# A new way to the first scores, a whole last copy and a new order table in an attention + SwiGLU kernel

## The chip, the core and the metric

The kernel runs on one core of a Trainium2 chip. Its engines are TensorE (PE in the profile; its weight loads are PEld), VectorE (DVE), ScalarE (ACT), GpSimd (POOL) and SyncE (SP), which issues most of the DMAs. The metric is the device time of one execution in microseconds (us); lower is better.

## The reference

With x of 2048 rows and 512 columns, 32 heads of 16, and a feed-forward width of 1792:

```
qkv    = x @ wqkv                                  # q, k, v per head
scores = q @ k.T * 16 ** -0.5                      # 32 heads, 2048 x 2048 each
a      = (softmax(scores) @ v) @ wo
b      = (silu(x @ w_gate) * (x @ w_up)) @ w_down
g      = sigmoid((x * gate_w).sum(-1))
out    = g * a + (1 - g) * b
```

All inputs and the output are bf16.

## The kernel before, in words

**Units and tiles.** Attention is cut into 32 units: four blocks of 512 queries (`QBW`) by eight groups of four heads. A unit has 16 tiles, one for each 128 keys. A tile holds the scores of four heads, 128 keys by 4 x 512 queries, and takes one of two ways:

- On ScalarE: two score pairs. Each is two matmuls into a PSUM tile `s_t` of 128x1024 and one exponential `e_t <- s_t` (`emit_pair`).
- On VectorE: four single scores `d_t` of 128x512. Each is evicted by a multiply-add to 16-bit integers that are read as bf16, which makes an approximate power (`emit_d`). The tile is then finished by whole-tile passes over `c_t` of 128x2048 (class `Pass`), of which GpSimd takes strips of columns (`strip`, `g_now`).

The products with the values go to `o_ps`, one PSUM tile for each unit (`pv`). A finished unit is copied out as `osb` (`post`). Its rows are gathered by DMA into `on`, which is normalised and multiplied by `wo`.

**Other work.** The q, k and v projections, the gate and up products `gu` with one tanh each on ScalarE (56 in all), and the down and output products `dps` and `ops` are chains of small pieces that fill TensorE between the score pairs (`Pacer`, `Chain`, `side`, `put_piece`).

**The order** is fixed when the program is built. A planner runs its own clock for each engine (`plan.pe`, `plan.dve`, `plan.act`, `plan.pool`) with fixed costs: 0.6 us for a VectorE eviction of 512 columns, 0.9167 us for an exponential (`ACT_US`). It decides step by step what each engine gets next. Each engine executes its instructions in that order. `v_unit` gives a tile to VectorE when, by the plan, VectorE would be done with it before ScalarE reaches the end of the unit (`plan.dve + busy + LEAD <= end`). So the number of exponentials is a result of the plan. The table `TURNS` bends the decisions: its letters come in twos for each score pair, the first read by `turn_of`, the second by `way_of`, and a dot changes nothing. For example, `k` or `j` puts value products ahead of other pieces, `h` and `i` move the limit in `v_unit` by 2 us, `v` and `w` change how much work may wait for VectorE, and `q` lets a GpSimd strip take 0.4 us longer. The table before has 131 letters besides the dots, 11 of them `q`.

**The way to the first scores** is written out by hand (L1245 to L1306). `keep_warm` issues products that nobody reads. `turn` transposes `x_rows` (kept in `wd_t`) by products with the identity. The other two of the four 128-column chunks of x come by DMA transposes. Chunk 3 goes to PSUM tile `tp` and is copied by ScalarE in one instruction of 1024 columns; chunk 2 is copied by VectorE in two of 512. Then come 8 matmuls for the keys (`kp0`, 1024 columns), 4 for the queries (`qp0`), and the largest key of each row on VectorE (`largest`, `k_neg`). After 32 small products for the first values (`v0`), `bound_add` adds the bound to `qp0`. VectorE makes two masked copies of the queries (`q0a`, one for each of two head pairs) and a plain one. ScalarE evicts the keys into `kaug` and the values into `vaug`. The first score pair reads `kaug` and the first masked copy. The planner starts after that, with `plan.dve = plan.pe + 3.9` (L1309).

**The end** is also written out by hand (L1765 to L1795). The last unit's `o_ps` is copied in two halves of 256 columns, the first by VectorE, the second by ScalarE (L1132 to L1136). Then `denominators` (tile `dt`), `recip16` and `spread_rows` (tile `rps`) run, four products `on_l = osb * rps`, and the last four matmuls with `wo_l`. The ten products listed in `rest` (tiles `al` and `al_o`) are put between these by `tail(n)`. Four evictions and three output DMAs end the program.

Nearly all instructions go through helpers, so that the profile shows L192 for PE, L195 for ACT and L204 for DVE, POOL and SP; they are told apart by their tiles.

Of the kernel before, what the change touches and what calls it, by code (L numbers as in the profile page):

```python
# [8 lines left out]
ACT = mybir.ActivationFunctionType  # L9
# [44 lines left out]
class Pacer:  # L54
# [33 lines left out]
    "..........s...j.....d........................r.......................q....b...s......l.........l"  # L88
    ".....n.y...f.x....a...b.................k........t............k...h........x...........g....a.s."
    ".......................t..................k...................o................................."  # L90
    "...r......k....................n...................q.....g................k..............r.m...."
    ".........w....................hq..........h...................o......y....d..n..k.....h........."
    "..hqj....xkt.y............a.c.....k....x....c.................................s...........o...j."
    ".......t....j.......i....x......c.s.......e.............j......................................."
    ".....q........................b..f......k.a...b....................................l............"
    "..............o...................................s............................................."
    "..........s........................r..............................................i.........j..."
    "..i............r..............................i............................r.....v........b....."
    ".....q...g..c...b.........h......n...ye..q...q...lc........w............a....w......iq.........."
    "..........b....................n..if.......t....c.............................d..............q.."  # L100
    "...............f.......v....h......u....k..m..cxk........v..................................e..."
    "...f..........j....q..................................o............w............kg.............."
    ".......g..................o"
# [4 lines left out]
def kernel(  # L108
# [176 lines left out]
    for g in (1, 2):  # L285
        ones_rows(nc.vector, g)
# [467 lines left out]
    def emit_pair(bs, ride=0):  # L754
# [1072 lines left out]
```

## Time and profile before

| | us |
|---|---|
| median of 3 runs | 748.87 (747.44 to 748.96) |
| the profiled execution, device time | 748.07 |
| its span, first to last instruction | 746.2 |
| first exponential of the scores starts | 12.92 |
| last exponential of the scores starts | 736.63 |
| last value products end | 738.10 |
| last output DMA is issued | 743.08 |

Busy time in the span: PE 725.7, DVE 724.0, ACT 730.5, POOL 278.5 us. The profile gives each instruction's start and duration; instructions on one engine overlap by a little, so the distance from start to start is what one costs in a dense stretch. The granted clock in the page is 1.00 throughout, but it is recorded only from the first change of clock on; before that, the spacing of the matmuls tells it.

### The profile page before, as it was taken

How to read it: one execution, taken by the hardware profiler on the slowest of the kernel's cores; microseconds unless marked ns; L12 is line 12 of the kernel's file. 1: busy time of each engine (PE TensorE's matmuls, PEld its weight loads, DVE VectorE, ACT ScalarE, POOL GpSimd, SP SyncE). 2: the span in 40 equal slices, each digit the busy share in tenths (PEclk: the TensorE clock that was granted, in tenths of full speed). 3: DMA queues.
4: the chain of work that ended last, by engine and by line, in shares of the span. 5: the costliest groups of instructions: out<-in, count | busy, mean ns of one | idle time of the engine just before them, and what ended most of it. 6: DMA issues, size and time to landing. Idle time of an engine off the chain costs nothing.

```text
span 746.2 us, 22814 instructions
## 1 busy us (share of the span) xinstructions
PE 725.7 (97%) x9173; PEld 214.7 (29%) x9173; DVE 724.0 (97%) x1242; ACT 730.5 (98%) x825; POOL 278.5 (37%) x348
## 2 busy tenths in 40 slices
PE   8999999999999999999999999999999999999997
PEld 3332222222222222322222232222222223222222
DVE  7899999999999999999999999999999999999995
ACT  5999999999999999999999999999999999999996
POOL 5222334333233254444334342342343255354320
PEclk9999999999999999999999999999999999999999
DMA  9000212244210012221100131312001132100001
GB/s 228 8 1 16 53 35 55 58 123 89 60 36 10 20 46 73 61 48 30 37 20 26 31 91 28 78 24 55 20 22 32 48 80 60 32 20 13 15 30 36
DMA packets 91026, 34.44 MB, mean 46 GB/s; under 512 B 75488, under 2 KB 90472, under 8 KB 90920
## 3 DMA queue, kind: packets, MB, share of 16 engines
q1 hardware_dynamic: 89192, 32.66, 18.2%
q8 instruction: 71, 1.16, 0.7%
q10 hardware_dynamic: 1728, 0.33, 0.2%
q14 instruction: 35, 0.29, 0.1%
HBM read 21.55 MB, written 2.35 MB: 32 GB/s over the span
## 4 chain that ended last, share of the span: by engine, by line
PE 54%; ACT 27%; DVE 12%; issue 7%; DMA 0%; ACTq 0%; DVEq 0%
ACT e_t L195 25%; PE s_t L192 18%; PE o_ps L192 15%; DVE c_t L204 7%; PE gu L192 6%; PE ops L192 5%; PE dps L192 2%; ACT th L195 2%; PE qp L192 2%; PE kp L192 2%; PE vp L192 2%; DVE mt L204 1%; DVE kaug L204 1%; DVE gs L204 1%; PE warm L192 1%
## 5 line engine op out<-in xcount | busy, mean ns | idle before, releaser
L195 ACT ACTIVATE e_t<-s_t 128x1024 bf16<-128x1024 f32 x756 | 707.1, 1094 | 1.9 <-PE s_t L192 1.1
L204 DVE TENSOR_SCALAR c_t<-d_t 128x512 uint16<-128x512 f32 x472 | 309.0, 683 | 2.4 <-PE d_t L192 1.9
L192 PE MATMUL s_t<-qx,kaug 32*128 32x512 bf16 (+1 forms) x1188 | 231.3, 384 | 7.9 <-ACT e_t L195 5.8
L204 POOL TENSOR_SCALAR c_t<-c_t 128x1088 uint16<-128x1088 uint16 (+14 forms) x203 | 147.8, 728 | 206.2 <-DVE c_t L204 147.6
L192 PEld LDWEIGHTS <-kaug 32*128 32x128 bf16 (+1 forms) x2048 | 81.9, 91 | 310.1 <-issue 306.2
L192 PE MATMUL o_ps<-e_t,vaug 128*32 128x512 bf16 (+2 forms) x1568 | 149.5, 378 | 0.3 <-DVE vaug L204 0.3
L192 PE MATMUL d_t<-qx,kaug 32*128 32x512 bf16 x444 | 145.3, 384 | 0.0
L192 PE MATMUL o_ps<-c_t,vaug 128*32 128x512 bf16 (+2 forms) x1352 | 121.6, 373 | 0.6 <-DVE vaug L204 0.3
L204 DVE TENSOR_SCALAR c_t<-c_t 128x2048 uint16<-128x2048 uint16 (+7 forms) x181 | 114.8, 646 | 0.5
L204 POOL TENSOR_TENSOR c_t<-c_t 128x480 bf16<-128x480 bf16 (+7 forms) x55 | 61.5, 1128 | 141.3 <-DVE c_t L204 93.3
L192 PEld LDWEIGHTS <-vaug 128*32 128x32 bf16 x3176 | 66.9, 95 | 108.5 <-issue 95.1
L192 PE MATMUL gu<-xT,wg 128*32 128x512 bf16 x896 | 72.2, 383 | 0.0
L192 PE MATMUL gu<-xT,wu 128*32 128x512 bf16 x896 | 67.8, 382 | 0.4
L192 PE MATMUL ops<-wd_t,mt 128*32 128x512 bf16 x672 | 56.5, 382 | 0.0
L204 DVE TENSOR_TENSOR c_t<-c_t 128x1568 bf16<-128x1568 bf16 (+10 forms) x51 | 47.8, 938 | 0.0
L192 PE MATMUL s_t<-q,kaug 32*128 32x512 bf16 (+1 forms) x192 | 37.4, 384 | 2.9 <-ACT e_t L195 2.6
L204 DVE SCALAR_TENSOR_TENSOR mt<-gs,gu 128x512 bf16<-128x512 bf16 x56 | 38.0, 679 | 0.3
L195 ACT ACTIVATE th<-gu 128x512 bf16<-128x512 f32 x56 | 38.2, 682 | 0.0
L204 DVE SCALAR_TENSOR_TENSOR gs<-th,gu 128x512 bf16<-128x512 bf16 x56 | 38.0, 679 | 0.1
L204 DVE TENSOR_SCALAR kaug<-d_t 128x512 uint16<-128x512 f32 x52 | 34.7, 682 | 0.5 <-PE d_t L192 0.5
L204 DVE TENSOR_SCALAR kaug<-c_t 128x2048 uint16<-128x2048 uint16 (+5 forms) x50 | 33.5, 669 | 0.1
L192 PEld LDWEIGHTS <-mt 128*32 128x32 bf16 (+1 forms) x1037 | 24.4, 95 | 26.9 <-issue 20.1
(150 smaller groups left out, 538.0 us busy)
## 6 DMA issues: line engine op xcount, KB each, us to landing
wg<-in_B_w_gate_dram SPq DMA_DIRECT2D x56, 128.0 KB
wu<-in_B_w_up_dram SPq DMA_DIRECT2D x56, 128.0 KB
on<-osb SPq DMA_DIRECT2D x120, 16.0 KB
rb<-rr SPq DMA_DIRECT2D x15, 128.0 KB
wd_t<-in_B_w_down_dram SPq DMA_DIRECT2D x7, 256.0 KB
qx<-qst SPq DMA_DIRECT2D x96, 16.0 KB
qx<-aq SPq DMA_DIRECT2D x96, 16.0 KB
out_dram<-o_t SPq DMA_DIRECT2D x12, 128.0 KB
```

Source lines behind the costliest of these rows:

```text
L192: return ordered(nc.tensor.matmul(*args, **kw))
L195: ordered(nc.scalar.activation(*args, **kw))
L204: return lambda *a, **kw: ordered(f(*a, **kw))
```

## The change

Four parts:

1. **The way to the first scores.** 8 products that nobody reads instead of 12 ahead of the transposing products, 2 instead of 1 behind them. Both transposed chunks are copied in halves, the first 512 rows by VectorE, the second by ScalarE. The memset of `kaug` group 2 (`ones_rows`) moves behind these copies. The keys are made in another order of matmuls, so that the first 512 columns are complete two matmuls earlier; the largest key is taken for each half and merged (`kpart0` has 4 columns). The queries are made in two halves of 256 columns in two PSUM tiles, and the bound is added to each half. One of the four masked half copies goes to ScalarE. The keys are evicted in two halves, the second behind that copy. 6 of the 8 value blocks come ahead of the bound, 2 behind. The eviction of the values moves from ScalarE to VectorE, behind the query copies.
2. **The last copy** of `o_ps` is one ScalarE instruction of 512 columns. For the 30 units between the first and the last, the small constant added in the copy is an immediate instead of a column read from `tiny`.
3. **The last products** in `tail`: 4, 2, 2 and 2 instead of 3, 3, 2 and 2, and the last two come ahead of the fourth of the last matmuls instead of the third.
4. **The table** `TURNS` has other letters throughout: 109 besides the dots, one of them `q`. New letters: `f` and `g` in the first place change the pacer's credit by 1.5, `d` and `o` in the second place let VectorE take a waiting score eviction, or the first due piece, ahead of a pass.

```diff
--- before.py
+++ after.py
@@ -85,22 +85,22 @@
 
 
 TURNS = (
-    "..........s...j.....d........................r.......................q....b...s......l.........l"
...
-    ".......g..................o"
+    ".......v.tbu.d.........r.........................d....b.................................k......."
...
+    ".......................n"
 )
 
 
@@ -282,8 +282,7 @@
             in_=wqk[:, :, i * D:i * D + 64].rearrange("p dc (j c) -> p dc j c", c=DH), func=ACT.Copy)
 
     pad(1)
-    for g in (1, 2):
-        ones_rows(nc.vector, g)
+    ones_rows(nc.vector, 1)
     ident = const.tile([P, P], BF16, name="ident")
     nc.gpsimd.memset(ident[:], 1.0)
     nc.gpsimd.affine_select(out=ident[:], in_=ident[:], pattern=[[-1, P]], compare_op=ALU.is_equal,
@@ -508,15 +507,12 @@
     def k_bound(b):
         vec.tensor_reduce(out=kb[:, b:b + 1], in_=kst[b][:, :], axis=AX.X, op=ALU.max, apply_absolute_value=True)
 
-    def v0(t0):
-
-        p = m_tile("vp")
-        for i in range(8):
+    def v0(p, t0, i0, i1):
+
+        for i in range(i0, i1):
             for dc in range(DC):
                 mm(p[:, 64 * i:64 * i + 64], lhsT=xT[:, dc, (t0 + i) * P:(t0 + i + 1) * P], rhs=wv[:, dc, 0:64],
                    start=(dc == 0), stop=(dc == DC - 1))
-        act(out=v0_out(t0), in_=p[:, :].rearrange("p (t h c) -> p t h c", h=4, c=DH), func=ACT.Copy)
-        m_free(p, 0.0)
 
     def v0_out(t0):
         return vaug[:, t0:t0 + 8, 0:4 * VC].rearrange("p t (h c) -> p t h c", c=VC)[:, :, :, 1:1 + DH]
@@ -777,6 +773,7 @@
         for b in bs:
             e_left[b] = pairs[0]
         pairs[0] += 1
+        pace.credit += {"f": 1.5, "g": -1.5}.get(turn_of(pairs[0]), 0.0)
 
     def turn_of(n):
 
@@ -1022,7 +1019,11 @@
                 j = next((j for j, v in enumerate(vops) if not v.poolable() and v.n // KT <= closed + AHEAD), 0)
                 vops.insert(0, vops.pop(j))
             fit = bool(vops) and not shut and not (code == "u" and vops[0].poolable()) and vops[0].n // KT <= closed + AHEAD and c_ready() <= now
-            if fit and vops[0].key != plan.last and (code == "m" or vops[0].n // KT < au and code != "l"):
+            if code == "d" and d_wait and d_wait[0][0] <= now + 0.05:
+                pay_d()
+            elif code == "o" and due:
+                pay(due[0])
+            elif fit and vops[0].key != plan.last and (code == "m" or vops[0].n // KT < au and code != "l"):
                 pay_v()
             elif d_wait and d_wait[0][2] // KT < au and d_wait[0][0] <= now + 0.05:
                 pay_d()
@@ -1124,18 +1125,14 @@
 
     def post(un):
         qb, g = UNIT[un]
-        if un < UNITS - 1:
-            osbs[un] = osb0[qb] if g == 0 else work.tile([P, QBW], BF16, tag="osb", name="osb")
+        osbs[un] = osb0[qb] if g == 0 else work.tile([P, QBW], BF16, tag="osb", name="osb")
         if un == 0:
             assert part_scaled
             vec.scalar_tensor_tensor(out=osbs[un][:, :], in0=o_of.pop(un)[:, :], scalar=tiny[:, 0:1], in1=o_part, op0=ALU.add, op1=ALU.add)
         elif un == UNITS - 1:
-            o, hw = o_of.pop(un), QBW // 2
-            osbs[un] = [work.tile([P, hw], BF16, tag=t, name="osb")[:, :] for t in ("osb", "th")]
-            vec.tensor_scalar(out=osbs[un][0], in0=o[:, 0:hw], scalar1=tiny[:, 0:1], scalar2=None, op0=ALU.add)
-            act(out=osbs[un][1], in_=o[:, hw:], func=ACT.Identity, bias=tiny[:, 0:1], scale=1.0)
+            act(out=osbs[un][:, :], in_=o_of.pop(un)[:, :], func=ACT.Identity, bias=tiny[:, 0:1], scale=1.0)
         else:
-            vec.tensor_scalar(out=osbs[un][:, :], in0=o_of.pop(un)[:, :], scalar1=tiny[:, 0:1], scalar2=None, op0=ALU.add)
+            vec.tensor_scalar(out=osbs[un][:, :], in0=o_of.pop(un)[:, :], scalar1=TINY, scalar2=None, op0=ALU.add)
 
     def settle(un):
         qb, g = UNIT[un]
@@ -1180,14 +1177,9 @@
                 normed.add((qb, b))
             at.setdefault(n0 + 13 + b, []).append(lambda norm=norm: later(0.345, norm))
 
-    def block(osb, tq):
-        if isinstance(osb, list):
-            osb, tq = osb[tq // 2], tq % 2
-        return osb[:, tq * P:(tq + 1) * P]
-
     def denominators(p, osb):
         for tq in range(TQ):
-            mm(p[:, 4 * tq:4 * tq + 4], lhsT=block(osb, tq), rhs=sel_t[:, :], start=True, stop=True)
+            mm(p[:, 4 * tq:4 * tq + 4], lhsT=osb[:, tq * P:(tq + 1) * P], rhs=sel_t[:, :], start=True, stop=True)
 
     def spread_rows(p, rt):
         for tq in range(TQ):
@@ -1242,15 +1234,13 @@
         return columns(NB + FC, "ops", lambda k: onc[qb][:, k, cs] if k < NB else mt[:, k - NB, cs],
                        lambda k: wo_t[:, k, :] if k < NB else wd_t[:, k - NB, :], lambda p: later(0.65, lambda: end(p)))
 
-    kp0 = ps_s.tile([P, 2 * QBW], F32, tag="s", name="kp0")
-    qp0 = m_tile("qp0")
     warm = ps_o.tile([P, QBW], F32, tag="o", name="warm")
 
     def keep_warm(n):
         for _ in range(n):
             mm(warm[:, :], lhsT=idle[:, 0:P], rhs=idle[:, :], start=True, stop=True)
 
-    kpart0 = const.tile([P, 3], F32, name="kpart0")
+    kpart0 = const.tile([P, 4], F32, name="kpart0")
     kneg0 = mt[:, 3, P:2 * P]
     kneg1 = mt[:, 3, 2 * P:3 * P]
     aq0 = mt[:, 2, :]
@@ -1274,34 +1264,56 @@
             mm(ps[k // TQ][:, k % TQ * P:(k % TQ + 1) * P], lhsT=x_rows[:, k, (dc - HALF) * P:(dc - HALF + 1) * P],
                rhs=ident[:, :], start=True, stop=True)
 
-    keep_warm(12)
+    HQ = QBW // 2
+    fore, aft = slice(0, QBW), slice(QBW, 2 * QBW)
+    keep_warm(8)
     tp = ps_s.tile([P, 2 * QBW], F32, tag="s", name="tp")
-    turn(DC - 1, [tp[:, 0:QBW], tp[:, QBW:2 * QBW]])
-    act(out=xT[:, DC - 1, 0:2 * QBW], in_=tp[:, :], func=ACT.Copy)
+    kp0 = ps_s.tile([P, 2 * QBW], F32, tag="s", name="kp0")
+    tps = [m_tile("tp") for _ in range(2)]
+    for i, dc in enumerate((DC - 1, DC - 2)):
+        turn(dc, [tp[:, i * QBW:(i + 1) * QBW], tps[i]])
+        vec.tensor_copy(out=xT[:, dc, fore], in_=tp[:, i * QBW:(i + 1) * QBW])
+        act(out=xT[:, dc, aft], in_=tps[i][:, :], func=ACT.Copy)
+        m_free(tps[i], 0.0)
     pad(0)
-    tps = [m_tile("tp") for _ in range(2)]
-    turn(DC - 2, tps)
-    for k in range(2):
-        vec.tensor_copy(out=xT[:, DC - 2, k * QBW:(k + 1) * QBW], in_=tps[k][:, :])
-        m_free(tps[k], 0.0)
-    keep_warm(1)
+    ones_rows(vec, 2)
+    keep_warm(2)
     arrived = (3, 0, 2, 1)
-    for dc in arrived:
+    for two in (arrived[:2], arrived[2:]):
         for tb in range(2):
-            mm(kp0[:, tb * QBW:(tb + 1) * QBW], lhsT=wpad[1][:, dc, :], rhs=xT[:, dc, tb * QBW:(tb + 1) * QBW],
-               start=(dc == arrived[0]), stop=(dc == arrived[-1]))
-    for dc in arrived:
-        mm(qp0[:, :], lhsT=wpad[0][:, dc, :], rhs=xT[:, dc, 0:QBW], start=(dc == arrived[0]), stop=(dc == arrived[-1]))
-    largest(0, kp0[:, :])
+            for dc in two:
+                mm(kp0[:, tb * QBW:(tb + 1) * QBW], lhsT=wpad[1][:, dc, :], rhs=xT[:, dc, tb * QBW:(tb + 1) * QBW],
+                   start=(dc == arrived[0]), stop=(dc == arrived[-1]))
+    qps = [m_tile("qp0") for _ in range(2)]
+    halves = [slice(i * HQ, (i + 1) * HQ) for i in range(2)]
+    for p, h in zip(qps, halves):
+        for dc in arrived:
+            mm(p[:, 0:HQ], lhsT=wpad[0][:, dc, :], rhs=xT[:, dc, h], start=(dc == arrived[0]), stop=(dc == arrived[-1]))
+    for i in range(2):
+        largest(i, kp0[:, i * QBW:(i + 1) * QBW])
+    vec.tensor_tensor(out=kpart0[:, 0:1], in0=kpart0[:, 0:1], in1=kpart0[:, 1:2], op=ALU.max)
     k_neg(kneg1, 0, idle[:, 0:P])
-    act(out=aq0, in_=qp0[:, :], func=ACT.Abs)
-    act(out=kaug[:, 0, 0:2 * QBW], in_=kp0[:, :], func=ACT.Identity, bias=onescol[:, 0:1], scale=1.0)
-    v0(0)
-    bound_add(qp0, kneg1, aq0)
+    for p, h in zip(qps, halves):
+        act(out=aq0[:, h], in_=p[:, 0:HQ], func=ACT.Abs)
+    act(out=kaug[:, 0, fore], in_=kp0[:, fore], func=ACT.Identity, bias=onescol[:, 0:1], scale=1.0)
+    vp0 = m_tile("vp")
+    v0(vp0, 0, 0, 6)
+    for p, h in zip(qps, halves):
+        bound_add(p[:, 0:HQ], kneg1, aq0[:, h])
+    v0(vp0, 0, 6, 8)
     for v in range(2):
-        vec.tensor_scalar(out=q0a[:, v, :], in0=qp0[:, :], scalar1=vsel[:, v:v + 1], scalar2=None, op0=ALU.mult)
-    vec.tensor_copy(out=q0_bf[0], in_=qp0[:, :])
-    m_free(qp0, plan.pe + 2.0)
+        for i, h in enumerate(halves):
+            if i > v:
+                act(out=q0a[:, v, h], in_=qps[i][:, 0:HQ], func=ACT.Copy, scale=vsel[:, v:v + 1])
+            else:
+                vec.tensor_scalar(out=q0a[:, v, h], in0=qps[i][:, 0:HQ], scalar1=vsel[:, v:v + 1], scalar2=None,
+                                  op0=ALU.mult)
+    act(out=kaug[:, 0, aft], in_=kp0[:, aft], func=ACT.Identity, bias=onescol[:, 0:1], scale=1.0)
+    for p, h in zip(qps, halves):
+        vec.tensor_copy(out=q0_bf[0][:, h], in_=p[:, 0:HQ])
+        m_free(p, plan.pe + 1.5)
+    vec.tensor_copy(out=v0_out(0), in_=vp0[:, :].rearrange("p (t h c) -> p t h c", h=4, c=DH))
+    m_free(vp0, plan.pe + 2.1)
     for g in (3, 4):
         ones_rows(vec, g)
 
@@ -1321,14 +1333,14 @@
                 vec.tensor_scalar(out=kaug[:, 0, tb * QBW:(tb + 1) * QBW], in0=p[:, :], scalar1=onescol[:, 0:1],
                                   scalar2=None, op0=ALU.add)
                 m_free(p, plan.dve)
-            later(0.67, lambda: largest(tb - 1, p[:, :]))
+            later(0.67, lambda: largest(tb, p[:, :]))
             later(0.6, evict)
         return columns(DC, "kp", lambda dc: wpad[1][:, dc, :], lambda dc: xT[:, dc, tb * QBW:(tb + 1) * QBW], end)
 
     def bound_all():
         def f():
-            k_neg(kneg0, 1, kneg1)
-            k_neg(kneg0, 2, kneg0)
+            k_neg(kneg0, 2, kneg1)
+            k_neg(kneg0, 3, kneg0)
         later(0.8, f)
 
     def q0_again(p):
@@ -1351,10 +1363,10 @@
             part_scaled.append(0)
         later(0.6, f)
 
-    second = [pace.add(k0_pieces(2), 1, -100), pace.add(k0_pieces(3), 1, -99)]
-    known = pace.add([(0.2, bound_all, False)], 2, -98, second)
+    second = [pace.add(k0_pieces(2), 2, -100), pace.add(k0_pieces(3), 2, -99)]
+    known = pace.add([(0.2, bound_all, False)], 3, -98, second)
     again = pace.add(columns(DC + 1, "qp", lambda k: wpad[0][:, k, :] if k < DC else kneg0,
-                             lambda k: xT[:, k, 0:QBW] if k < DC else aq0, q0_again), 2, -97, [known])
+                             lambda k: xT[:, k, 0:QBW] if k < DC else aq0, q0_again), 3, -97, [known])
     v_late = pace.add(v0_pieces(8), 2, 5, [known])
     parts = pace.add(columns(1, "rp", lambda k: sbc_t, lambda k: ratio, scale_part), 3, 11, [again], 1,
                      cond=lambda: part_done and ratio_done and ratio_done[0] <= plan.pe)
@@ -1765,21 +1777,21 @@
     assert not at
     un = UNITS - 1
     osb = osbs[un]
-    tail(min(3, len(rest)))
+    tail(min(4, len(rest)))
     dt = m_tile("dt")
     denominators(dt, osb)
     rt = work.tile([P, 4 * TQ], BF16, tag="rt", name="rt")
     recip16(rt[:, :], dt[:, 0:4 * TQ])
-    tail(min(3, len(rest)))
+    tail(min(2, len(rest)))
     rps = ps_s.tile([P, 2 * QBW], F32, tag="s", name="rps")
     spread_rows(rps, rt)
     tail(min(2, len(rest)))
     on_l = work.tile([P, QBW], BF16, tag="rd", name="on_l")
     for tq in range(TQ):
         cs = slice(tq * P, (tq + 1) * P)
-        vec.tensor_tensor(out=on_l[:, cs], in0=block(osb, tq), in1=rps[:, cs], op=ALU.mult)
+        vec.tensor_tensor(out=on_l[:, cs], in0=osb[:, cs], in1=rps[:, cs], op=ALU.mult)
     for tq in range(TQ):
-        if tq == 2:
+        if tq == 3:
             tail(len(rest))
         mm(a_ps[tq][:, 0:D], lhsT=on_l[:, tq * P:(tq + 1) * P], rhs=wo_l[:, 1, :], start=False, stop=True,
            skip_group_check=tq < 2)
```

More of the change, by code (lines that the diff above doesn't have):

```diff
@@ L87 @@
 TURNS = (
-    "..........s...j.....d........................r.......................q....b...s......l.........l"
[L89 to L102, printed above, removed]
```

14 lines of the change are left out of this document (added).

## The prediction

> **What bounds the kernel now.** I read first the page's busy shares, then the stretches (busy time by engine), then the groups, and last the timeline of the start and of the end.
>
> ```profile
> PE 725.7 (97%) x9173; PEld 214.7 (29%) x9173; DVE 724.0 (97%) x1242; ACT 730.5 (98%) x825; POOL 278.5 (37%) x348
> ```
>
> Three engines are full at once. The stretches say where they are not (columns: length, then busy time and instructions of PE, PEld, DVE, ACT, POOL):
>
> ```profile
> 12.92:30.00 17.08, 16.27 (x206) 5.54 (x207) 13.78 (x26) 16.83 (x19) 1.10 (x1) 1.00 0.37 115
> ...
> 300.00:400.00 100.00, 98.33 (x1264) 28.44 (x1260) 99.89 (x171) 99.87 (x114) 42.03 (x48) 1.00 0.16 39
> ...
> 700.00:738.00 38.00, 37.63 (x468) 11.25 (x464) 34.71 (x58) 37.57 (x41) 9.81 (x10) 1.00 0.08 25
> ```
>
> From 12.92 on, ScalarE is never idle for more than 0.4% of a hundred microseconds. So the time is three terms: the way to the first exponential (12.92), the work that ScalarE is given (756 exponentials and 56 tanh), and the end behind it. The change touches all three. The groups that price it:
>
> ```profile
> L195 ACT ACTIVATE e_t<-s_t 128x1024 bf16<-128x1024 f32 x756 | 707.1, 1094 | 1.9 <-PE s_t L192 1.1
> L204 DVE TENSOR_SCALAR c_t<-d_t 128x512 uint16<-128x512 f32 x472 | 309.0, 683 | 2.4 <-PE d_t L192 1.9
> ...
> L204 DVE TENSOR_SCALAR osb<-o_ps,tiny 128x512 bf16<-128x512 f32 x30 | 22.3, 743 | 0.6 <-PE o_ps L192 0.6
> ```
>
> The first and second are on the page, the third is in the list of VectorE's groups by form. 17 exponentials in a row took 15.69 us in the timeline, 0.92 each.
>
> **The start, step by step.** The timeline, with start, duration and the idle time before:
>
> ```profile
> 1.25 4.73 PE L192 MATMUL warm<-mt 128*128 128x512 bf16 x12 [1.25 <-DVE mt L253]
> 5.82 1.06 PE L192 MATMUL tp<-ident,wd_t 128*128 128x128 bf16 x16
> 6.72 0.38 PE L192 MATMUL warm<-mt 128*128 128x512 bf16 x1
> ```
> ```profile
> 9.47 1.23 DVE L204 TENSOR_REDUCE kpart<-kp 128x1 f32<-128x1024 f32 x1 [1.49 <-PE kp L192]
> 10.73 0.35 DVE L204 SCALAR_TENSOR_TENSOR mt<-mt,kpart 128x128 bf16<-128x128 bf16 x1
> 11.69 1.41 DVE L204 TENSOR_SCALAR mt<-qp,vsel 128x512 bf16<-128x512 f32 x2 [0.61 <-PE qp L192]
> ```
>
> (a) Fewer products. Their weight loads stand 0.43 us apart up to 5.07, so eight end at 1.25 + 8 x 0.43 = 4.67 in place of 5.82. But then the data is late: 54 of the 1024 packets of 512 bytes that carry `x_rows` moved after 4.5 us (DMA view in half microseconds). The 512 packets of the first `wqk` load were done but for 11 at 4.5, and ScalarE was released by it at 5.30. With the same lag `x_rows` is there at 5.45. Gain 0.37, not 1.15.
>
> (b) From the first transposing product to the keys: before 5.82 to 7.55, 1.73 us, since one ScalarE copy of 1024 columns (1.02) stood between. After: 16 products at 0.056 and two warm ones at 0.215 make 1.35. The half copies hide beside that: VectorE's first is done 1.12 behind the first product, ScalarE's (0.60 for 512 columns, row of the first values) at 1.25 and needed at 1.8. Keys start at 6.80. Gain 0.38. The DMA transpose of chunk 1 ends its packets at 7.08 and with the lag is there at about 7.8; the sixth key matmul wants it at 7.88, so nothing more is to be had here.
>
> (c) From the keys to the bound: before 7.55 to 11.16, 3.61. After: the first half is complete after 6 matmuls, 1.45 behind the start, VectorE takes two reductions of 0.65 (row of the later halves, 0.63 and 0.68), a merge of some 0.1 (no row; 0.06 by the small memsets, 0.15 by the gate column's eviction), and `k_neg` 0.35: 3.32 with the hand-overs. TensorE needs 8 x 0.215 + 8 half products at 0.11 + 24 x 0.029 = 3.3 and is level. The moved memset (0.91) fits on VectorE between its copies (end 7.3) and the first reduction (8.25) with nothing to spare. Gain 0.29.
>
> (d) From the bound to the scores: before 11.16 to 12.49. After: halves come out at 10.54 and 10.65; VectorE's first masked half (0.48, row of the 256-column `osb`) ends at 11.0, ScalarE's at 11.2, scores at 11.25. Gain 0.20. But ScalarE then evicts the second key half (0.65) and begins the first exponential at 11.87 where scores plus 0.43 (12.49 to 12.92) would allow 11.68: 0.19 is given back.
>
> Sum: 0.37 + 0.38 + 0.29 + 0.20 - 0.19 = **1.05 us**, first exponential at 11.87. The second wants VectorE's other masked halves (11.9 + 0.5), in time for 12.8. The value eviction now stands behind 0.8 of query copies on VectorE and ends at 13.4; its first reader ran at 16.09. The two memsets behind it end at 15.3, before 15.84. The bounds: 0 if something later holds the start of the dense stretch, 1.3 if (d) gives nothing back.
>
> **The end.** Two engines copy the halves of `o_ps` one after the other, not beside each other: VectorE 738.14 to 738.62, ScalarE 738.66 to 739.13.
>
> ```profile
> 738.14 0.48 DVE L204 TENSOR_SCALAR osb<-o_ps,tiny 128x256 bf16<-128x256 f32 x1 [3.29 <-PE o_ps L192]
> ```
> ```profile
> 738.66 0.47 ACT L195 ACTIVATE osb<-o_ps,tiny 128x256 bf16<-128x256 f32 x1 [1.00 <-DVE osb L204]
> ```
>
> One copy of 512 takes 0.69 (the row of `a_l_a`, same form with a column operand), so it ends at 738.83: 0.30 earlier. The four products put ahead end at 738.89, and all four `denominators` now stand behind the copy where two did: some 0.07 back. The last `al_o` still has five products ahead of it from the first `on_l` on, so the moved two change the third eviction, not the fourth. Gain **0.23**, bounds 0.10 and 0.35.
>
> **The immediate.** 743 against 683 ns: 60 ns x 30 = 1.8 us less on VectorE. ScalarE is the one that is full, so this is worth nothing if ScalarE's list stays, and 1.8 if VectorE alone held it. A tile moved off ScalarE costs it two exponentials, 1.84, and VectorE four evictions and about 1.7 of passes, 4.4: 1.8 us shared that way is 1.8 / (1 + 4.4 / 1.84) = 0.5. I take **0.5**.
>
> **The table.** No row shows it. What it can do is move tiles, at 1.84 us of ScalarE each. Within 300 to 700 VectorE and ScalarE are both 99.7% full, so neither way is free; I take 0, with two tiles either way as bounds (3.7).
>
> The sum is 1.05 + 0.23 + 0.5 = 1.78. From the profiled execution's 748.07 (span and 1.87 around it) that is 746.3, from the median 748.87 it is 747.1. Two of the three runs lie near the median: I say **746.9**. What a measurement can tell here is about 0.2%, 1.5 us: faster is below 747.4, slower above 750.4.
>
> **Rivals.**
>
> 1. *More exponentials (slower).* The new table has one `q` where the old has 11. Each let GpSimd take 0.4 us more of a strip, 480 columns by its rows (1088 columns 1.10, 352 columns 0.48), and VectorE passes 480 columns in 0.16 (0.685 for 2048). Ten make 1.6 us more for VectorE and cancel the immediate. Where that turns the test in `v_unit`, tiles stay on ScalarE. One tile (758 exponentials) makes 746.9 + 0.5 + 1.84 = 749.2, two 751.1. It is slower from 760 exponentials on. For it: VectorE has no room in the middle. Against: it idles 3.3 us in 12.92 to 30 and 3.3 ahead of the last copy.
> 2. *Fewer exponentials.* Those idle stretches are used: one tile 745.1, two 743.2.
> 3. *A late clock.* Matmuls were 0.43 us apart until 5.07 and 0.215 after, TensorE having run without a gap since 1.25. After the change it stands still from 4.67 to 5.45. If the clock then rises only after another such stretch from 5.45 on, at 9.5, the transposing products take 1.7, the warm ones 0.86 and the first key matmuls 0.43 each: the keys end at 10.5 instead of 8.5, and the 2.0 us take the whole start back: 748.9. Against: no row shows that a short gap matters.
> 4. *The gain of the start is absorbed*, because the later DMA transposes (packets until 12.35) reach the second key blocks no earlier: 748.0.
>
> [...]
>
> **Chances.** Forecast 0.44 (746.0 to 748.0); rival 2 0.17; rival 1 0.26; rival 3 0.08; rival 4 0.05. Faster: 0.35 of the forecast and rival 2, 0.52. Same: the forecast's rest, rivals 3 and 4, and 0.05 of rival 1, 0.27. Slower: 0.21. The range leaves the outer part of rivals 1 and 2 out: 744.3 to 751.0.
>
> **What would show it.** First transposing product at 5.45 with spacing 0.056 (not 0.107); key matmuls at 6.8; first exponential at 11.9; the count of exponentials at 756; `osb` at 683 ns; from the last value product to the last output DMA 4.75 us instead of 4.98. A count off by two or more, or a start above 12.5, would make the prediction wrong.

## The result and the profile after

The changed kernel takes 750.6 us (median of 16 runs, 748.89 to 751.72), the kernel before 748.27 on the same chips. The ratio is 1.0028, 95% interval 1.0020 to 1.0037: slower by 0.28%, where 746.9 against 748.87, 0.26% faster, was forecast. The profiled execution is one of the shortest, 749.18 us with a span of 747.4 (before: 748.07 and 746.2). Each run lists its mean granted clock: 1.00 in 4 of the 16 runs (spans 747.2 to 747.6), 0.996 to 0.998 in 7 (748.4 to 749.2), 0.995 in 5 (749.2 to 750.0). Before, all listed runs have 0.999 or 1.00. This mean is taken from the first recorded change of clock on, so that a late first rise does not show in it: the profiled execution has 1.00, though its weight loads stood 0.43 us apart up to 10.47. So two things are to be found: 1.2 us of span in the profiled execution, and one to three more that most other runs lose.

The profiled execution first. From the page:

```profile
L195 ACT ACTIVATE e_t<-s_t 128x1024 bf16<-128x1024 f32 x756 | 706.6, 1098 | 1.1 <-PE s_t L192 0.6
```

The count of exponentials is the same, 756. The two traces differ in five stretches (us; together 1.26 up to the last output DMA):

| stretch | before | after | difference |
|---|---|---|---|
| start to the first exponential | 12.92 | 14.98 | +2.06 |
| first to sixth exponential | 4.91 | 4.65 | -0.26 |
| sixth to last exponential | 718.79 | 717.97 | -0.82 |
| last exponential to the end of the last value product | 1.48 | 2.14 | +0.66 |
| from there to the last output DMA | 4.98 | 4.60 | -0.38 |

The start is the loss. The timeline of TensorE in the changed kernel, with VectorE's first copy (start, duration, idle time before and what ended it; dots stand for lines between):

```profile
1.25 3.59 PE L192 MATMUL warm<-mt 128*128 128x512 bf16 x8 [1.25 <-DVE mt L253]
5.71 1.03 PE L192 MATMUL tp<-ident,wd_t 128*128 128x128 bf16 x8 [0.86 <-DMA wd_t<-in_A_x_dram]
6.36 0.69 DVE L204 CAST xT<-tp 128x512 bf16<-128x512 f32 x1 [1.88 <-PE tp L192]
...
7.10 1.01 PE L192 MATMUL tp<-ident,wd_t 128*128 128x128 bf16 x8 [0.35 <-DVE xT L204]
...
8.76 2.77 PE L192 MATMUL kp<-xT,mt 128*128 128x512 bf16 x8
```

The eight products end, TensorE waits 0.86 us for `x_rows`, does half of the transposing products, and waits again, for 0.35 us, for VectorE's copy out of the other half of the same tile `tp`: a wait that is new and was not foreseen. Eight key matmuls then take 2.77 us where they took 1.89. The weight loads beside them show why:

```profile
10.04 0.15 PEld L192 LDWEIGHTS <-mt 128*128 128x128 bf16 x1 [0.28 <-issue]
10.47 1.65 PEld L192 LDWEIGHTS <-mt 128*128 128x128 bf16 x11 [0.28 <-issue]
```

They stand 0.43 us apart, 0.15 each, up to 10.47; the clock's record begins at 10.54 (before: 5.28). The full clock came 5.3 us later.

What most other runs lose, this execution does not show. Its late start even hides one loss: the first pieces that read `wqk` reach TensorE at 16.38 and wait for nothing.

```profile
16.38 0.93 PE L192 MATMUL kp<-xT,wqk 128*32 128x512 bf16 x12
```

Runs of the experiments, which start earlier, show it.

### The profile page after: what moved, and what is told of

Its sections match the earlier page's. It is cut to its first block, busy times and chain, and to the rows that moved or that the text cites. A ratio compares the mean times of both kernels' runs of the same rounds, so it can differ in the third digit from the quotient of the medians.

```text
span 747.4 us, 22900 instructions
## 1 busy us (share of the span) xinstructions
PE 726.6 (97%) x9214; PEld 216.0 (29%) x9214; DVE 723.5 (97%) x1247; ACT 730.5 (98%) x828; POOL 277.5 (37%) x345
## 4 chain that ended last, share of the span: by engine, by line
PE 49%; ACT 27%; DVE 16%; issue 7%; DMA 1%; ACTq 0%; DVEq 0%
ACT e_t L195 25%; PE s_t L192 17%; PE o_ps L192 14%; DVE c_t L204 10%; PE ops L192 6%; PE gu L192 6%; DVE mt L204 2%; PE qp L192 2%; ACT th L195 2%; PE kp L192 1%; DVE gs L204 1%; DVE kaug L204 1%; PE vp L192 1%; DMA wd_t<-in_A_x_dram 1%; DVE on L204 1%
## 5 line engine op out<-in xcount | busy, mean ns | idle before, releaser
L204 DVE TENSOR_SCALAR c_t<-d_t 128x512 uint16<-128x512 f32 x444 | 290.8, 680 | 3.0 <-PE d_t L192 2.4
L204 POOL TENSOR_SCALAR c_t<-c_t 128x1088 uint16<-128x1088 uint16 (+14 forms) x154 | 108.5, 705 | 170.4 <-DVE c_t L204 137.3
L204 POOL TENSOR_TENSOR c_t<-c_t 128x480 bf16<-128x480 bf16 (+7 forms) x69 | 81.5, 1192 | 204.5 <-DVE c_t L204 127.0
L192 PE MATMUL d_t<-qx,kaug 32*128 32x512 bf16 x440 | 148.9, 384 | 0.4 <-DVE qx L204 0.3
L192 PE MATMUL o_ps<-c_t,vaug 128*32 128x512 bf16 (+2 forms) x1424 | 127.4, 370 | 0.0
L204 DVE TENSOR_SCALAR c_t<-c_t 128x2048 uint16<-128x2048 uint16 (+5 forms) x196 | 124.8, 648 | 0.7
L204 DVE TENSOR_SCALAR kaug<-d_t 128x512 uint16<-128x512 f32 x88 | 58.2, 680 | 0.1
L204 DVE TENSOR_TENSOR c_t<-c_t 128x1568 bf16<-128x1568 bf16 (+12 forms) x61 | 56.2, 921 | 0.0
L204 POOL TENSOR_SCALAR c_t<-kaug 128x352 uint16<-128x352 uint16 (+12 forms) x42 | 31.5, 751 | 29.6 <-DVE c_t L204 23.7
L204 POOL TENSOR_SCALAR kaug<-c_t 128x352 uint16<-128x352 uint16 (+11 forms) x36 | 27.7, 769 | 27.7 <-DVE c_t L204 21.1
```

Of the source, the lines that this page charges most:

```text
L192: return ordered(nc.tensor.matmul(*args, **kw))
L204: return lambda *a, **kw: ordered(f(*a, **kw))
```

## The experiments

In all of them VectorE and ScalarE execute the changed kernel's instructions in its order behind the start, but for e2 and e8, and for the copies that e13 and e14 change. A few products that nobody reads are added on TensorE in e7 and e12. Most runs stand on one profiled execution, so the positions in us are of that one.

**e1: the four products put back.**

```diff
-    keep_warm(8)
+    keep_warm(12)
```

> The changed kernel with 12 products that nobody reads ahead of the transposing products, as before the change, in place of 8; nothing else differs. Theory A (the clock): the gap between the eighth product and the arrival of x_rows keeps the matmuls at 0.43 us until about 10.5; without the gap the spacing falls to 0.215 at about 5.3, the keys start at 8.1 in place of 8.8 and end at 9.8 in place of 11.9, the first exponential starts at 13.1 in place of 14.98, and the time is 747.6. Theory B (the new way's own waits: the second transposing products behind VectorE's first copy, the merge of two reductions, ScalarE's extra copy): the clock makes no difference to the end, the first exponential stays at 14.5 or later and the time at 750 or more.

Measured: 752.4 us (ratio 1.0043, 1.0030 to 1.0055), clock 0.994 or 0.995 in all five runs. Theory A got the start half right: the clock rose at 5.97, the keys started at 8.21, the first exponential at 13.55, 1.43 earlier than in the changed kernel (13.1 was expected). And yet the span is 750.8, 3.4 longer. Neither theory had that. The loss lies between the first and the sixth exponential, at 13.55 and 22.40.

**e2: the kernel before, with four products fewer.**

```diff
-    keep_warm(12)
+    keep_warm(8)
```

> The kernel before with 8 products in place of 12; all else is as before. Theory A: TensorE stands still from 4.67 to about 5.6, the clock rises only near 10.5, eight key matmuls at 0.43 end at about 11.0 in place of 9.4, first exponential at 14.4 in place of 12.92, time 749.8 to 750.3. Theory B: the four products were waste, first exponential at 12.9 or a little earlier, time 748.2.

Measured: 748.31 us (0.9996, 0.9987 to 1.0005), first exponential 12.88. In the profiled execution theory A is wrong: the gap is there (0.65 us of wait for `x_rows`), but the clock rose at 6.12. So a gap of this size need not hold the clock back. That it never does is not shown: three of the eleven runs have spans of 747.7 to 747.9, above all 17 of the kernel before on that chip (746.0 to 747.3), and their traces were not kept. A late rise would fit them.

**e3: the changed kernel with the old start.** The part from `keep_warm(8)` to the memsets is replaced by the old one, and the planner's state set to what the new one leaves:

```diff
...
+    banks[:] = [1.78, 2.38, 1.78]
+    plan.pe = 0.14
```

> The changed kernel with the way to the first scores as before (part 1 undone), with the planner's state behind it set to what the new way leaves, so that everything after the start is the changed kernel's instruction for instruction. It shows what the table, the immediate and the end are worth by themselves. By the two traces the dense stretch is 1.1 us shorter and the end 0.2 longer: first exponential at 12.9, time 747.4. If a table that was not planned for this start costs, 749 or more.

Measured: 751.87 us (1.0035, 1.0023 to 1.0047). The first exponential is at 12.92, as before the change, and the time is still the long one, in five of six runs: the second loss does not need the new start. The stretches of this run, with the bounds put where the clock changed (columns: length, busy time and instructions of PE, PEld, DVE, ACT, POOL, then the granted clock, the DMA share and GB/s):

```profile
12.09:15.50 3.41, 1.50 (x8) 0.39 (x7) 3.09 (x5) 2.90 (x4) 0.00 (x0) 1.00 0.96 288
15.50:22.32 6.82, 5.97 (x44) 1.19 (x44) 1.69 (x3) 2.78 (x4) 0.00 (x0) 0.50 0.53 157
```

TensorE is busy for 1.50 of 3.41 us, and then runs at half clock for 6.83 us, in which ScalarE works 2.78 us instead of all the time. Before the change the same stretch had 2.75 busy:

```profile
12.11:15.52 3.41, 2.75 (x34) 0.85 (x33) 3.08 (x5) 2.66 (x4) 0.00 (x0) 1.00 1.00 293
```

What TensorE waits for is in its timeline of e3:

```profile
14.31 0.39 PE L192 MATMUL kp<-xT,wqk 128*32 128x512 bf16 x2
16.35 1.46 PE L192 MATMUL kp<-xT,wqk 128*32 128x512 bf16 x10 [1.65 <-DMA wqk<-in_A_wqkv_dram]
17.75 0.61 PE L192 MATMUL s_t<-mt,kaug 64*128 64x512 bf16 x2
```

Before the change the first pieces behind the third score pair's place were those of the first group's second keys (`kp<-xT,mt`, 20 matmuls at 13.48); pieces that read `wqk` came at 17.64, when its load was in. The diff moves the release of the former from tile 1 to tile 2 (`k0_pieces(2), 2`). For one tile the planner has nothing but the next group's key pieces, and issues them at 14.31, when 448 KB of `wqk` are still coming. TensorE takes its pieces in the order of the program: the fourth scores stand behind them and come at 17.75, before the change at 15.54.

**e5: no wait between the transposing products.** Twelve products, and a tile of its own for the second chunk's first half (the planner's state is set as in e3, here and in e6, e7 and e11 to e14):

```diff
...
-        turn(dc, [tp[:, i * QBW:(i + 1) * QBW], tps[i]])
+        tf = m_tile("tp") if i else tp[:, 0:QBW]
+        turn(dc, [tf, tps[i]])
...
```

> As e1_after_12warm, and the first half of the second transposed chunk goes to a PSUM tile of its own in place of the other half of tp, so that its products need not wait for VectorE's copy out of tp. The instructions after the start are unchanged. Theory A with the wait as a second term: keys start at 7.2, first exponential at 12.3, time 746.8. Theory B says the same wait is all there is: it would show here alone, and not in e1_after_12warm. If ScalarE's or VectorE's copies bind instead, keys start at 7.6 or later and the first exponential at 12.7 to 13.1.

Measured: 751.56 us (1.0032, 1.0019 to 1.0044). Keys at 7.35, 0.86 earlier than e1, and first exponential at 12.69. From the first transposing product to the keys it is 1.32 us where e1 took 2.04, so the wait in `tp` was worth 0.72; the other 0.14 is an earlier first product. Theory A's 12.3 and 746.8 were missed: an earlier start only makes the wait for `wqk` longer (2.03), and the clock fell in all six runs.

The trace shows one more wait for a whole tile. The keys' matmuls were put in another order so that VectorE could begin with the first 512 columns of `kp0` after six of them. It begins at 9.28, right behind the eighth, after 0.46 of waiting:

```profile
7.35 1.89 PE L192 MATMUL kp<-xT,mt 128*128 128x512 bf16 x8
```
```profile
9.28 1.29 DVE L204 TENSOR_REDUCE kpart<-kp 128x1 f32<-128x512 f32 x2 [0.46 <-PE kp L192]
```

e1, e3 and e5 made theory C: the pieces released out of turn wait for their weights, and a TensorE that is idle for much of a stretch loses its clock (it was busy for 1.50, 1.50 and 1.24 of the 3.41 us ahead of the fall). It was tried in several ways, against theory D, that the new order is worse all along.

**e6: the load earlier by one place.** On SyncE's queue, the rest of the key weights ahead of the rest of the value weights, e5 otherwise:

```diff
-    queue.dma_start(out=wv[:, :, 64:D], in_=A_wqkv[:, 2 * D + 64:3 * D].rearrange("(dc p) c -> p dc c", p=P))
     for c0 in (D, 0):
+        if c0 == 0:
+            queue.dma_start(out=wv[:, :, 64:D], in_=A_wqkv[:, 2 * D + 64:3 * D].rearrange("(dc p) c -> p dc c", p=P))
         queue.dma_start(out=wqk[:, :, c0 + 64:c0 + D],
```

> As e5_12warm_own_tile, with one pair of loads swapped on SyncE's queue: the rest of the key weights (wqk, 448 KB) ahead of the rest of the value weights (rb, 448 KB). No engine's instructions change. Theory C: in the changed kernel the pieces of the second key blocks are released one tile later, so that the first pieces to reach TensorE are those that read wqk; they stand waiting for that load (2.0 us in e5_12warm_own_tile, 14.1 to 16.5), TensorE is busy in only 36% of that stretch, the clock halves from 15.9 to 22.8, and ScalarE waits 4.7 us for scores. Then the load, 1.3 us earlier, takes away the wait or all but 0.8 of it; the clock stays at 1.0, the sixth exponential starts at 17.4 to 17.9 in place of 22.0, and the time is 747.2. Theory D (the new order is worse all along): 750.5 or more, clock or not.

Measured: 749.48 us (1.0011, 1.0002 to 1.0021); sixth exponential at 20.03 in place of 22.02. The wait is 1.05 in place of 2.03. It is not gone, and the clock still fell, for one stretch of 3.41 us instead of two:

```profile
12.26:15.67 3.41, 1.64 (x16) 0.46 (x16) 3.08 (x7) 3.16 (x4) 0.00 (x0) 1.00 1.07 317
15.67:19.08 3.41, 3.41 (x30) 0.60 (x26) 0.51 (x1) 1.37 (x2) 0.00 (x0) 0.50 0.95 290
```

Half of what theory C expected; the load was later than its sum had it. In three of the twelve runs the clock was 0.999 or 1.00, with spans of 746.0 to 746.3.

**e7: the wait kept, the clock held.**

```diff
+            if dc == 0 and tb == 0 and not kst:
+                keep_warm(7)
```

> As e5_12warm_own_tile, with 7 products that nobody reads (1.5 us) put on TensorE ahead of the first piece that reads wqk. The wait for the load stays (until 16.5), and TensorE is busy in 80% of that stretch in place of 36%. This parts the wait from the clock. Theory C with the clock as the larger term: the clock stays at 1.0, scores and key pieces behind the wait run at full speed, the sixth exponential at 19.4, time 749.0. If the wait itself is the cost and the half clock is hidden under ScalarE: sixth exponential at 21 or later, time 751 or more.

Measured: 749.23 us (1.0020, 1.0009 to 1.0031). This parts the two. The sixth exponential is at 20.07, between theory C's 19.4 and the rival's 21. The load still ends the wait, at 16.93, but the work behind it runs at full speed:

```profile
16.93 0.82 PE L192 MATMUL kp<-xT,wqk 128*32 128x512 bf16 x10 [1.28 <-DMA wqk<-in_A_wqkv_dram]
17.69 0.39 PE L192 MATMUL s_t<-mt,kaug 64*128 64x512 bf16 x2
```

10 matmuls in 0.82 us where e5 took 1.46. From the end of the wait to the sixth exponential it is 3.14 us, where e5 took 5.51 (16.51 to 22.02): the half clock alone was worth 2.4 us. The wait stays. Two stretches busy for 2.31 and 2.13 us did not lower the clock. In three of twelve runs it still fell (clock 0.997, 752 us), so the filling did not hold it in every run.

**e8: the old releases, in the changed kernel.**

```diff
-    second = [pace.add(k0_pieces(2), 2, -100), pace.add(k0_pieces(3), 2, -99)]
+    second = [pace.add(k0_pieces(2), 1, -100), pace.add(k0_pieces(3), 1, -99)]
...
```

> The changed kernel with the releases of the second key blocks, of the merged bound and of the queries' second pass as before (1, 2 and 2 in place of 2, 3 and 3), nothing else. The planner makes another order of the whole from it, with the same table. Theory C: no wait for wqk at the start. But by the program it has 772 exponentials in place of 756, so that 16 x 0.92 = 14.7 us are added: about 762. It shows what a table is worth that was not made for its kernel; the sixth exponential tells of the start, at 4.9 behind the first.

Measured once: 766.95 us, 772 exponentials, first at 12.82, sixth at 18.85. Releases moved by one tile make the planner keep 16 more pairs on ScalarE. Table and releases are a pair, and the undoing of one says nothing of its worth. No piece waits for `wqk` at the start, as theory C had it (the first pieces are `kp<-xT,mt` again, at 14.24); but the sixth exponential, 6.0 behind the first, was not where theory C had it (4.9), because the clock fell in this run too (at 14.13; mean granted clock 0.996), as in e10 below without a long wait for the load.

**e10: the changed kernel, with e6's swap of the loads and nothing else.**

> The changed kernel as it is, with the loads swapped as in e6_keys_weights_first and nothing else. Theory C: the wait for wqk is gone whatever the start does, and the clock does not fall back (1.0 in all runs, where the changed kernel had 1.0 in 4 of 16). What stays is the late rise of the clock in the runs where the gap behind the eighth product spoils a stretch: first exponential between 12.8 and 15.0. Time 747.0 where the clock rises in time, 749.1 where not, median 748.3. Theory D: 750 or more.

Measured: 749.04 us (1.0011, 1.0002 to 1.0019). By the two ratios the swap alone takes some 1.3 us off the changed kernel. But the clock was below 0.999 in 7 of 12 runs, where theory C expected none: with the start's own waits, none over 0.42, the stretch ahead of 14.14 was busy for 1.98 of 3.41 us and the clock fell, though the wait for `wqk` was only 0.18.

```profile
10.73:14.14 3.41, 1.98 (x30) 0.83 (x26) 2.88 (x8) 3.04 (x5) 0.89 (x1) 1.00 1.01 237
14.14:17.55 3.41, 3.23 (x24) 0.65 (x22) 1.97 (x3) 2.01 (x3) 0.00 (x0) 0.50 1.04 320
```

Yet an earlier stretch of the same run was busy for less, 1.88, and the clock stayed full behind it:

```profile
3.90:7.32 3.42, 1.88 (x21) 1.14 (x20) 1.44 (x7) 1.50 (x5) 3.03 (x13) 1.00 1.28 265
```

**e11: the load ahead of the four late transposes.** e5, with

```diff
     for t0 in (0, 2 * QBW):
+        if t0:
+            queue.dma_start(out=wqk[:, :, D + 64:2 * D],
+                            in_=A_wqkv[:, D + 64:2 * D].rearrange("(dc p) c -> p dc c", p=P))
...
```

> As e5_12warm_own_tile, with the rest of the key weights loaded ahead of the last four DMA transposes of x (they came behind them and behind the value weights); the instructions of the other engines are unchanged. In e6_keys_weights_first the load still came 1.05 us late and the stretch ahead of 15.7 was 48% busy, so the clock fell once. Theory C: here the load is there by about 10, no piece waits for it, every stretch of 3.4 us is at least 60% busy and the clock stays at 1.0; first exponential at 12.5, sixth at 17.2, from there on the 717.96 us to the last exponential that three kernels with this order took, end 9.85 behind it: span 745.0, time 746.8, so the changed kernel would be faster than before by 0.2%. If the transposes, now 1.7 us later, hold the second key blocks, the sixth exponential is at 18 or later and nothing is won.

Measured: 746.98 us (0.998, 0.9971 to 0.9989), clock 0.999 or 1.00 in all runs. Time, span (745.2) and sixth exponential (17.34) are what theory C expected within 0.2 us; the first exponential, 12.80, is 0.3 later. No piece waits for the load:

```profile
14.20 0.83 PE L192 MATMUL kp<-xT,wqk 128*32 128x512 bf16 x12
14.96 0.39 PE L192 MATMUL s_t<-mt,kaug 64*128 64x512 bf16 x2
```
```profile
12.73:16.14 3.41, 2.69 (x30) 0.74 (x28) 3.08 (x6) 3.41 (x5) 0.00 (x0) 1.00 1.03 268
```

So the changed order, table and end are worth 0.2% when TensorE's weights are there, and this version beats both kernels. Theory D falls. e5 loses 4.8 us against this run between the first and the sixth exponential (9.33 and 4.54), about half by the half clock (e7) and half by the wait. The early load was not tried in the changed kernel with its eight products.

**e12: the small waits filled as well.**

```diff
     v0(vp0, 0, 6, 8)
+    keep_warm(1)
...
+        if pairs[0] in (1, 2):
+            keep_warm(1)
```

> As e11_keys_weights_ahead, with one product that nobody reads (0.22 us) in each of the three waits of TensorE before the first, the second and the third score pair (0.30, 0.30 and 0.42 us). If stretches of less than 0.6 busy are what lowers the clock, this holds it at 1.0 in all runs, wherever the stretches fall; time 746.8 with little spread. If e11_keys_weights_ahead is at 1.0 already, the two are the same; each product that does not fit costs up to 0.2.

Measured: 747.14 us (0.9981, 0.9972 to 0.9990), clock 0.999 or 1.00: the same as e11. There was nothing left to hold.

**e13: the immediate undone**, on e12.

```diff
-scalar1=TINY
+scalar1=tiny[:, 0:1]
```

> As e12_ahead_and_filled, with the small constant read from its column again in the 30 copies of the units (743 ns each in place of 683), nothing else. The sum took the immediate at 0.5 us, bounds 0 and 1.8. The distance from the sixth to the last exponential tells it without the noise of the start: 717.96 if it is worth nothing, 718.5 at 0.5, 719.8 if VectorE alone holds the order.

Measured: 747.43 us (0.9989, 0.9980 to 0.9997). Sixth to last exponential 718.67, against 718.00, 718.01 and 718.01 in e12, e11 and e14: the immediate is worth 0.67 us of the 1.8 that it takes off VectorE (the medians, 0.29 apart, do not tell the two runs apart). ScalarE's instructions are the same in both; the 0.67 comes in small steps all along the stretch. The groups of VectorE by form, of the changed kernel and of e13:

```profile
L204 DVE TENSOR_SCALAR osb<-o_ps 128x512 bf16<-128x512 f32 x30 | 20.4, 680 | 0.3 <-PE o_ps L192 0.3
```
```profile
L204 DVE TENSOR_SCALAR osb<-o_ps,tiny 128x512 bf16<-128x512 f32 x30 | 22.2, 740 | 0.3 <-PE o_ps L192 0.3
```

The kernel before took 718.79 for the same stretch, and 719.02 in e2, which has its order: the new order by itself gives 0.12 to 0.35, about as much as those two traces of one order differ (0.23).

**e14: the old end**, on e12: the two-engine copy, `tail` 3, 3, 2, 2 and the last two ahead of the third matmul.

> As e12_ahead_and_filled, with the end as before: the last copy in two halves on two engines, the last products 3, 3, 2 and 2, the last two ahead of the third of the last matmuls. The sum took the new end at 0.23 us. From the end of the last value product to the last output DMA: 4.59 in the changed kernel, 4.98 before; if that is the new end's doing, this run shows 4.9 to 5.0 and a span 0.3 to 0.4 longer than e12_ahead_and_filled; if it comes from where the order put the first rows' products, 4.6.

Measured: 747.23 us (0.9981, 0.9973 to 0.9990), not to be told from e12 by its time. The trace tells it: last value product to last output DMA 5.00 us against 4.60, so the new end is worth 0.40. The old form waited for VectorE first:

```profile
737.97 0.47 ACT L195 ACTIVATE osb<-o_ps,tiny 128x256 bf16<-128x256 f32 x1 [1.62 <-DVE osb L204]
```

The new form, in the changed kernel:

```profile
739.80 0.69 ACT L195 ACTIVATE osb<-o_ps,tiny 128x512 bf16<-128x512 f32 x1 [1.10 <-PE o_ps L192]
```

The 0.66 us more ahead of it (last exponential to last value product, 2.14 in e12 and e14 alike) come from the new order, which puts ten matmuls of the first rows' products (`a_l_a`, `a_l_b`) between the last scores and the last value products, where six stood before.

## Why the prediction was wrong

**The step that failed** is the sum of the start, "1.05 us", "first exponential at 11.87", with its lower bound "0 if something later holds the start of the dense stretch", and the table taken at 0 with only tiles as bounds. The profiled execution began its first exponential at 14.98, and the runs that begin it earlier lose 4 to 5 us before the sixth (e1, e3 and e5 against e11). Three things were missing in the sum; a fourth, step (c) below, was in it and did not come.

1. *The releases.* They stand in the diff and were given no price. One tile later for the second key blocks makes other pieces first in TensorE's queue. Asking what is next, and when its weights land, would have shown it: in the trace before, `wqk` pieces come at 17.64 and their load's packets run until after 15. The wait itself (1.54 to 2.03 us in e1, e3 and e5) is a loss below the bound of 0.
2. *The clock falling back.* Rival 3 had the clock, but only in its rise at the start, at 0.08, "no row shows that a short gap matters". With the wait for `wqk`, TensorE was busy in 36% (e5) to 48% (e6) of the 3.41 us ahead of the fall, and 3.41 (e6) or 6.83 us (e1, e3, e5) at half clock followed. That is the 2.4 us between e5 and e7. In e10 the clock fell behind the start's own short waits, none over 0.42 us, and 0.18 of wait for the load; in e8, where no piece waits for `wqk` at the start, the mean granted clock was 0.996 as well. By their granted clock 12 of the 16 runs of the changed kernel fell back too; their traces were not kept, so which of the two did it there is not shown.
3. *The clock rising late.* This is rival 3 as written, and the profiled execution shows it: keys end at 11.5 where "10.5 instead of 8.5" was said, first exponential 14.98. The gap that was named need not do it (e2 has 0.65 us of it, and its profiled execution rose at 6.12). After the first rise the changes of the clock lie whole steps of 3.41 us apart: in e1 it rose at 5.97, fell at 16.21 and rose at 23.04, which are 3 and 2 times 3.41. That the steps hold ahead of the first rise as well is assumed here and not shown. Counted back so from the rise at 10.54, the first two stretches held 2.46 and 2.19 us of work (the 1.00 behind them is no reading, since the record begins at 10.54):

```profile
0.30:3.71 3.41, 2.46 (x6) 0.87 (x7) 2.10 (x20) 0.91 (x1) 3.09 (x10) 1.00 0.36 84
3.71:7.12 3.41, 2.19 (x12) 1.04 (x11) 1.34 (x6) 1.36 (x4) 3.04 (x12) 1.00 1.29 266
```

   The gap and the second wait, the one in `tp`, both lie in the second. In e10, with the same two waits (0.98 and 0.56 us, here 0.86 and 0.35), the stretch ahead of the rise at 3.90 began 0.19 later than the first one here and held 2.65. That where the stretches fall made the difference between these two executions is the author's estimate from 2.65 and 2.46; what decides the rise, and whether the wait in `tp` was needed too, is not shown.

**The other steps.**

(a) `x_rows` at 5.45: it was 5.43 to 5.71 in the runs with eight products. Right.

(b) Keys at 6.80: with the clock in time and no wait in `tp`, 7.35 in e5 and 7.46 in e11, where the first transposing product was at 6.03 and 6.13; from there 1.32 and 1.33 us against 1.35. The step was right, but it overlooked that PSUM tile `tp` was waited for as a whole; e1 and e5 put that at 0.72.

(c) Keys to bound, said 3.32 against 3.61 before: 3.85 in e5, e10 and e11. This step failed: it gained 0.29 on paper and cost 0.24. VectorE was to begin 1.45 behind the keys' start, after six matmuls; it began at 1.93, after all eight, as before (1.92), and the second reduction and the merge (0.16) then came on top. `kp0` was waited for as a whole, like `tp`.

(d) Bound to first exponential, said to gain 0.01 in all: 1.49 in e5 and e11 against 1.76 before, a gain of 0.27. ScalarE's second key eviction gave nothing back. So from the keys on, 5.34 was measured where 5.07 was said. With 12.69 (e5) and 12.80 (e11) against 12.92 the new start is worth 0.1 to 0.2 where the clock holds, not 1.05; these runs keep the twelve products, so that what (a) promised is not in them.

*The end*, said 0.23 (0.10 to 0.35): 0.40. Right in mechanism, too small.

*The immediate*, said 0.5 (0 to 1.8): 0.67. The size was right by luck: the 0.5 was worked out from tiles moving off ScalarE, with nothing to gain "if ScalarE's list stays". In e13 the list stayed, and the 0.67 was there.

*The table*, said 0: 0.12 to 0.35 better in the dense stretch and 0.66 worse ahead of the end. Rivals 1 and 2, more or fewer exponentials, did not happen: 756 in both. e8 shows how far that is from safe (772). Rival 4 looked at the right loads' queue, but at the transposes instead of `wqk`.

Open: what a stretch must hold. Busy time alone does not decide it. Stretches with 1.24 to 1.98 us of 3.41 lowered the clock and those with 2.13 or more did not, but the one with 1.88 in e10 did not either. A first rise came behind 2.65 (e10) and, counted back as above, not behind 2.46; but after the fall in e5 a stretch with 2.83 was followed by half clock again:

```profile
15.93:19.34 3.41, 2.83 (x20) 0.53 (x20) 0.37 (x1) 0.78 (x1) 0.00 (x0) 0.50 0.94 284
```

e7 still lost the clock in three runs whose traces were not kept.

## What to carry to other kernels

When a release or a place in a queue moves, ask which piece is then first in line on its engine, and when its data lands: a transfer that was in time before can become the wait (`wqk` here, 1.54 to 2.03 us in e1, e3 and e5). When work is split in halves, see in a trace whether the reader waits for its half or for the whole tile. A wait of TensorE cost as much again behind it here (2.03 us of wait in e5 and, against e7, 2.4 us by the half clock that followed), so look at how busy it is in stretches of a few microseconds, not at the longest gap alone. And compare the granted clock of several runs before trusting the one that was profiled.

## What the runs showed of the hardware

- TensorE's clock halved after stretches of 3.41 us in which it was busy for 1.24 to 1.98 us, in e10 with no wait over 0.42 us (another stretch of that run, with 1.88, kept it); it stayed half for 3.41 us (e6, e10) or 6.83 us (e1, e3, e5), and that cost 2.4 us in e5 against e7.
- After the first rise its changes lay whole steps of 3.41 us apart (10.24 and 6.83 us in e1, 10.24 and 3.41 in e10). The first rise came at 3.90 in e10 and at 10.54 us in the changed kernel, though the first product started at 1.25 in both: behind a stretch with 2.65 us busy in e10, and, counted back, not behind one with 2.46 in the changed kernel. The runs of the changed kernel have spans 2.8 us apart (747.2 to 750.0); that the place of the stretches explains it is an estimate from these two rises.
- A [128, 1] column as the added scalar makes a VectorE copy of 128x512 out of PSUM 740 ns long, an immediate 680 (e13 and the changed kernel).
- Twice here a reader or writer of one half of a PSUM tile waited for the work on the whole tile: 0.72 us in `tp` (e1 against e5), and in e5 VectorE began 1.93 us behind the keys' start in `kp0` where six of the eight matmuls would have allowed about 1.45, an estimate from their spacing.
